# One ScalarE operation as the seed of the inverse root, and an earlier place for tile 0's scaled table

## The chip, the cores and the metric

The program runs on one core of a Trainium2 chip. Its time is the device time of one execution in microseconds (us). Of the kernel before there are three timed runs, with a median of 675.24 us (674.69 to 675.34), and one profiled execution.

The engines are named as the profile names them: PE is TensorE (PEld its weight loads), DVE is VectorE, ACT is ScalarE, POOL is GpSimd, SP is SyncE, which issues most transfers.

## The reference, cut to what matters

```python
def _layernorm(x, axis=-1, eps=1e-5):
    m = jnp.mean(x, axis=axis, keepdims=True)
    v = jnp.var(x, axis=axis, keepdims=True)
    return (x - m) / jnp.sqrt(v + eps)

# x: [1, 2048, 640]; w_r, w_i: [2048, 321]; w_gate, w_up: [640, 1728]; w_down: [1728, 640]
def _A_ref(x, w_r, w_i):                      # spectral filter
    X = jnp.fft.rfft2(x, axes=(-2, -1))
    return jnp.fft.irfft2(X * (w_r + 1j * w_i), s=(S, D), axes=(-2, -1))

def _B_ref(x, w_gate, w_up, w_down):          # gated unit without a nonlinearity
    return ((x @ w_gate) * (x @ w_up)) @ w_down

h  = x + _A_ref(_layernorm(x), w_r, w_i)
h2 = h + _B_ref(_layernorm(h), w_gate, w_up, w_down)
```

## The kernel before, in words

**Stages.** The 2048 rows are held as 16 tiles X[0] to X[15] of 128 x 640. Stage 1 (up to 38.91 us in the profile) is the first layernorm and the first part of the Fourier transform; then come the filter, the inverse transform, and from about 152 us the second layernorm, which overlaps with the inverse transform's end and the gated unit. The gated unit fills the rest, with PE busy nearly all the time.

**Stage 1, tile by tile.** For tile t four things are needed before its matmuls (`s1_mm`, recorded as L252, 14 records a tile). (1) The statistics: mean and variance by `bn_stats` and `bn_aggr` on DVE (L176, L179, L180), or, for eight of the tiles, two passes over the tile on ACT: a sum (L195) and a sum of squares (L196), each followed by an accumulator read. (2) The inverse root r = (v + eps)^-1/2 (`inverse_root`, L201): ACT takes a square root (L205), DVE a reciprocal (L206) as seed, and three small DVE operations (L207 to L209) make one Newton step, r (1.5 - 0.5 r^2 (v + eps)). (3) The folds of the tile: sums and differences of mirrored columns (L229 `odd`, L234, L238, L239 `even`). L234 needs the mean and writes the part that the first matmuls read, L239 the part that the later ones read. (4) The table of cosines and sines scaled by r (`scale_c`, tile name bits): on ACT (L267) for tile 0 and tiles 5 to 15, on DVE (L269) for tiles 1 to 4. So r does not scale the data but the small table that they are multiplied with. ACT also copies the results out of PSUM (L275, L278). POOL makes a few of the odd folds.

**Groups.** The roots are taken for several tiles at once: tile 0, tile 1, tiles 2 and 3, 4 and 5, 6 to 9, 10 and 11, 12 and 13, 14 and 15. The statistics of 0, 2, 3, 12 and 13 come wholly from DVE; for those groups L183 forms v + eps as an operation of its own. Groups with ACT passes get v + eps out of the scaling of the sum of squares (L198). The second layernorm has four groups more (`scale_shift`, L748).

**What sets the order.** Each engine does its instructions in the order in which the program issues them. In the loop over tiles (L318 to L377) that order is written by hand for tiles 0 to 2; from tile 3 on `weave` places the root's steps between the folds by fixed costs. An instruction that waits holds up all behind it on its engine. Tiles are numbered by t; in the instruction lists the data of tile t is x_68 for t = 0, x_69 for t = 1, and so on (x_77 is tile 9, x_78 is tile 10).

Of the kernel before, what the change touches and what calls it, by code (L numbers as in the profile page):

```python
# [11 lines left out]
F32 = mybir.dt.float32  # L12
F32R = mybir.dt.float32r
AF = mybir.ActivationFunctionType
OP = mybir.AluOpType

P = 128
# [23 lines left out]
EPS = 1e-5  # L41
# [37 lines left out]
def tile_spectral_glu(ctx: ExitStack, tc: tile.TileContext, x, wre, wim, wgu, wlast, wdown, wdlast,  # L79
                      cc, ci, fmain, frem, imain, irem, mm, out):  # L80
    nc = tc.nc

    keep = ctx.enter_context(tc.tile_pool(name="keep", bufs=1))
    work = ctx.enter_context(tc.tile_pool(name="work", bufs=8))
    small = ctx.enter_context(tc.tile_pool(name="small", bufs=5))
# [3 lines left out]
    tt, act = nc.vector.tensor_tensor, nc.scalar.activation  # L89
# [10 lines left out]
    def bank(tag, bufs=2):  # L100
        return pools["y" if tag in ("im2", "ir2") else "a"].tile([P, 512], F32, tag=tag, name=tag, bufs=bufs)
# [10 lines left out]
    def wk(shape, name):  # L112
        return work.tile(shape, F32, tag="wk", name=name)
# [51 lines left out]
    def moments(ts, junk=None, total=None, k=0):  # L165
        n = len(ts)
        m2 = small.tile([P, n], F32, tag="m2", name="m2")
        ve = small.tile([P, n], F32, tag="ve", name="ve")

        def statistics(ts):  # L170
            n = len(ts)
            mv = small.tile([P, n, 2], F32, tag="mv", name="mv")
            fs, late = [], None
            for i, t in enumerate(ts):
                st = small.tile([P, 2, 6], F32, tag="st", name="st")
                fs.append(lambda st=st, t=t: nc.vector.bn_stats(st[:, 0], X[t][:, 0:320]))  # L176
                if late:
                    fs.append(late)
                fs.append(lambda st=st, t=t: nc.vector.bn_stats(st[:, 1], X[t][:, 320:640]))  # L179
                late = lambda st=st, i=i: nc.vector.bn_aggr(mv[:, i], st)  # L180
            fs.append(late)
            fs.append(lambda: nc.vector.tensor_scalar(m2[:, 0:n], mv[:, :, 0], 2.0, None, op0=OP.mult))
            fs.append(lambda: nc.vector.tensor_scalar(ve[:, 0:n], mv[:, :, 1], EPS, None, op0=OP.add))  # L183
            return fs

        if junk is None:
            return m2, ve, statistics(ts)
        first = statistics(ts[:k]) if k else []
        sq = small.tile([P, n], F32, tag="sq", name="sq")
        fs = []  # L190
        if total is not None:
            fs.append(lambda: nc.vector.tensor_scalar(m2, total, 2.0 / D, None, op0=OP.mult))
        for i, t in list(enumerate(ts))[k:]:
            if total is None:
                fs.append(lambda t=t, i=i: act(junk[i], X[t], AF.Identity, scale=2.0 / D, accum_out=m2[:, i:i + 1]))  # L195
            fs.append(lambda t=t, i=i: act(junk[i], X[t], AF.Square, bias=m2[:, i:i + 1], scale=-2.0,  # L196
                                           accum_out=sq[:, i:i + 1]))
        fs.append(lambda: nc.vector.tensor_scalar(ve[:, k:n], sq[:, k:n], 0.25 / D, EPS, op0=OP.mult, op1=OP.add))  # L198
        return m2, ve, first + fs

    def inverse_root(ve, r, n):  # L201
        sd = small.tile([P, n], F32, tag="sd", name="sd")
        w = small.tile([P, n], F32, tag="w", name="w")
        return [
            lambda: act(sd, ve, AF.Sqrt),  # L205
            lambda: nc.vector.reciprocal(r, sd),  # L206
            lambda: nc.vector.scalar_tensor_tensor(w, r, -0.5, r, op0=OP.mult, op1=OP.mult),  # L207
            lambda: tt(w, w, ve, op=OP.mult),
            lambda: nc.vector.scalar_tensor_tensor(r, w, 1.5, r, op0=OP.add, op1=OP.mult),  # L209
        ]  # L210

# [2 lines left out]
    def front(ts, k):  # L214
        n = len(ts)
        r = small.tile([P, n], F32, tag="r", name="r")
        junk = [fold[:, o:o + D] for o in (NR * 1026, NR * 1026 + D)]
        m2, ve, fs = moments(ts, junk * 2 if k < n else None, k=k)
        for i, t in enumerate(ts):
            SC[t] = r[:, i:i + 1], m2[:, i:i + 1]  # L220
        return fs, inverse_root(ve, r, n)

    def folded(t):
        o = t % NR * 1026
# [39 lines left out]
    def scale_c(t):  # L264
        CR[t] = crs[t % 4]
        if t in SCALE_ON_ACT:
            act(CR[t], cct, AF.Copy, scale=SC[t][0])  # L267
        else:
            nc.vector.tensor_scalar(CR[t], cct, SC[t][0], None, op0=OP.mult)  # L269
# [4 lines left out]
    def s1_rest(t):  # L274
        act(at(rest, t), PS1[t][1][:, 0:P].rearrange("p (g m) -> p g m", g=32), AF.Copy)  # L275
# [14 lines left out]

    warm = wk([P, P], "warm")
    nc.vector.memset(warm, 0.0)
    pw = bank("re")
    for n in range(16):
        nc.tensor.matmul(pw[:, 0:P], warm, warm, start=True, stop=True)
    f0, c0 = front((0,), 1)
    f1, c1 = front((1,), 0)
    for f in f0:
        f()
    for ts, when, aside, root in GROUPS:  # L300
        k = len(when)
        fs, cs = front(ts, k)
# [15 lines left out]
    for t in range(NT):  # L318
        if t == 1:
            nc.gpsimd.dma_start(frall, frem)  # L320
        if t >= 1:
            fs = even(t)
            if t + 1 < NT and t + 1 not in ASIDE:
                fs.insert(1, (0.4, lambda: odd(t + 1, nc.vector)))
            if t < AHEAD:
                fs.insert(1 + (t <= 2), (0.2, lambda: scale_c(t)))
            if t == 1:
                fs, (recip, w, *left) = fs[1:], dve[1][0]
                for f in (c1[4], fs[0][1], fs[1][1], recip, fs[2][1], w):
                    f()  # L330
                dve[2].insert(0, left)
            elif t == 2:
                (ww, r), = dve[2]
                for f in (fs[0][1], ww, tail[2].pop(), fs[1][1], r, fs[2][1], fs[3][1]):
                    f()
            else:
                weave(fs, dve[t], t in FOLDS)
            for f in tail[t]:
                f()
            if t < AHEAD - 1:  # L340
                s1_rest(t - 1)
                main = lambda: s1_main(t - 1, PS1[t - 1][0], 0, 4)
                for f in acts[t][:1] + post[t] + ([*acts[t][1:], main] if t < 2 else [main, *acts[t][1:]]):
                    f()
            else:
                s1_main(t - 1, PS1[t - 1][0], 0, 4)
                s1_rest(t - 1)
                for f in post[t]:
                    f()
                if t + 1 in SCALE_ON_ACT:  # L350
                    scale_c(t + 1)
                for f in acts[t]:
                    f()
        else:
            e0 = [f for _, f in even(0)]
            c0[0]()
            for f in (e0[0], c0[1], e0[1], c0[2], c0[3], e0[2], c0[4], *f1[:-1]):
                f()
        if t in FOLDS:
            nc.gpsimd.tensor_copy(small.tile([P, 1], F32, tag="hold", name="hold"), folded(t)[1][:, 383:384])  # L360
            for k in FOLDS[t]:
                odd(k, nc.gpsimd)
        if t >= 1:
            for f in stats[t]:
                f()
            if AHEAD <= t + 1 < NT and t + 1 not in SCALE_ON_ACT:
                scale_c(t + 1)
        else:
            scale_c(0)
            b2a, b2, b3a, a2, b3, a3, m, v = stats[0]  # L370
            for f in (b2a, b2, b3a, b3, a2, f1[-1], acts[0][0], c1[0], *acts[0][1:], even(1)[0][1], a3, c1[1], m, c1[2],
                      v, c1[3]):
                f()
        if t == 0:
            for f in post[0]:
                f()
        s1_mm(t)  # L377
# [370 lines left out]
    def scale_shift(ts, junk, total=None):  # L748
        n = len(ts)
        r = small.tile([P, n], F32, tag="r", name="r")  # L750
        b = small.tile([P, n], F32, tag="b", name="b")
        m2, ve, fs = moments(ts, junk, total)
        cs = inverse_root(ve, r, n)
        cs.append(lambda: nc.vector.scalar_tensor_tensor(b, m2, -0.5, r, op0=OP.mult, op1=OP.mult))
        for i, t in enumerate(ts):
            SC[t] = r[:, i:i + 1], b[:, i:i + 1]
        return fs, cs
# [101 lines left out]
    total = small.tile([P, 8], F32, tag="total", name="total", bufs=1)  # L859
# [6 lines left out]
    for ts in (range(3), range(3, 6), range(6, 8)):  # L866
        n, t0 = len(ts), ts[-1] + 1
        fs, cs = scale_shift(ts, [scrap] * n, total[:, ts[0]:t0])
# [301 lines left out]
    for n, (blk, p) in enumerate(steps):  # L1170
        if p == 6:
# [121 lines left out]
            if blk == 0:  # L1293
                fs, cs = scale_shift(range(8, 16), None)
# [6 lines left out]
        if prev[1] == 6:  # L1301
            fs = [[lambda j=j, prev=prev: down(*prev, j)] for j in range(8)]
            slots = [dict(zip(range(4, 8), fs[0:3] + [fs[3] + fs[4]])), dict(zip((2, 3, 4), fs[5:]))]
        else:
            fs = down_products(*prev, (0, 1)) + down_products(*prev, (2, 3))
# [222 lines left out]
```

## Time and profile before

| | |
|---|---|
| median of three runs | 675.24 us (674.69 to 675.34) |
| the profiled execution, its own time | 674.77 us |
| its span in the profile | 673.0 us |
| PE busy | 662.0 us (98%) |
| PEld busy | 587.0 us (87%) |
| DVE busy | 471.6 us (70%) |
| ACT busy | 322.7 us (48%) |
| POOL busy | 393.6 us (58%) |

The span begins at the first instruction and ends at the last; 1.77 us of the run lie around it. The shares are means over stages that are limited by different engines, so that the stage which the change touches has to be looked at by itself. The granted TensorE clock is at its full level in all 40 slices of the span.

### The profile page before, as it was taken

The page shows a single profiled execution, that of the slowest core. Times are in us where ns is not written, and L with a number is a line of the kernel's source. Part 1 is how long each engine was busy: PE and PEld are TensorE (multiplying, and loading weights), DVE is VectorE, ACT ScalarE, POOL GpSimd, SP SyncE. Part 2 cuts the span into 40 slices and gives each one's busy share as a digit, 9 for nine tenths or more (in the row PEclk, how much of TensorE's full clock was granted, in tenths as well). Part 3 has the DMA queues.
Part 4 walks back from the last instruction along what each step waited for, and adds up shares of the span by engine and source line. Part 5 has one row for each costly group of instructions (what it writes and reads, how often), then busy time and mean ns, then how long its engine had stood idle before and what let it go on. Part 6 is the DMA issues. An engine that isn't in the chain of part 4 may idle for free.

```text
span 673.0 us, 10263 instructions
## 1 busy us (share of the span) xinstructions
PE 662.0 (98%) x3695; PEld 587.0 (87%) x3695; DVE 471.6 (70%) x967; ACT 322.7 (48%) x622; POOL 393.6 (58%) x377
## 2 busy tenths in 40 slices
PE   6999999999999999999999999999999999999997
PEld 6999998887898888888888899888888888888887
DVE  6969996788757868594857567754747575756654
ACT  6977774585525244463626246634434252525220
POOL 3101124650297987878787544188787878787610
PEclk9999999999999999999999999999999999999999
DMA  9639884502212110042332458212002121212004
GB/s 317 226 104 283 242 256 142 170 1 79 78 40 78 40 70 23 27 119 59 96 81 79 98 125 265 79 40 76 11 32 79 40 78 40 79 40 80 1 1 156
DMA packets 48953, 66.12 MB, mean 98 GB/s; under 512 B 24082, under 2 KB 30670, under 8 KB 48774
## 3 DMA queue, kind: packets, MB, share of 16 engines
q1 hardware_dynamic: 48246, 62.91, 30.3%
q0 software_dynamic: 288, 2.16, 0.8%
q8 instruction: 29, 0.48, 0.3%
q10 hardware_dynamic: 368, 0.39, 0.3%
q14 instruction: 22, 0.18, 0.1%
HBM read 54.61 MB, written 10.84 MB: 97 GB/s over the span
## 4 chain that ended last, share of the span: by engine, by line
PE 92%; DMA 4%; DVE 2%; ACT 1%; issue 1%; SPq 0%; DVEq 0%; ACTq 0%
PE e L119 49%; PE d L119 26%; PE eo L119 4%; PE re L119 2%; PE u L455 2%; PE y L119 2%; PE im L119 2%; PE im L507 2%; DMA x<-in_x_dram 2%; PE im L252 1%; DMA bits<-in_mm_dram 1%; PE ir L507 1%; DMA wts<-in_wre_dram 1%; PE y L773 0%; ACT xt L783 0%
## 5 line engine op out<-in xcount | busy, mean ns | idle before, releaser
L119 PE MATMUL e<-xt,wst 128*128 128x512 f32 x864 | 213.2, 391 | 0.0
L119 PEld LDWEIGHTS e<-xt,wst 128*128 128x128 f32 x864 | 159.8, 188 | 30.6
L1047 DVE TENSOR_TENSOR x<-d,x 128x320 f32<-128x320 f32 x280 | 123.4, 484 | 51.6 <-PE d L119 47.5
L119 PE MATMUL d<-wd,ht 128*128 128x320 f32 x832 | 143.6, 308 | 0.0
L119 PEld LDWEIGHTS d<-wd,ht 128*128 128x128 f32 x832 | 131.1, 188 | 7.6
L961 POOL TENSOR_TENSOR wst<-raw,wst 128x1024 fp32r<-128x1024 f32 x23 | 55.5, 2412 | 66.9 <-ACT wst L960 49.0
L119 PE MATMUL e<-t,wst 128*128 128x512 f32 x360 | 94.3, 392 | 0.0
L119 PEld LDWEIGHTS e<-t,wst 128*128 128x128 f32 x360 | 66.3, 188 | 12.6
L119 PE MATMUL d<-wt,ht 128*128 128x320 f32 x360 | 69.5, 310 | 0.0
L977 POOL TENSOR_TENSOR wst<-raw,wst 128x896 fp32r<-128x896 f32 (+1 forms) x46 | 65.1, 1439 | 0.2 <-ACT wst L972 0.2
L119 PEld LDWEIGHTS d<-wt,ht 128*128 128x128 f32 x360 | 57.3, 188 | 2.3
L1063 ACT ACTIVATE ht<-e 128x512 fp32r<-128x512 f32 x44 | 26.4, 600 | 51.4 <-DVE e L1126 25.8
L1102 ACT ACTIVATE h<-e 128x512 f32<-128x512 f32 x24 | 14.3, 596 | 67.2 <-PE e L119 67.2
L1022 DVE TENSOR_TENSOR x<-d,x 128x320 f32<-128x320 f32 x62 | 27.5, 485 | 23.2 <-PE d L119 23.2
L658 ACT ACTIVATE wd<-draw 128x320 fp32r<-128x320 f32 (+1 forms) x30 | 15.7, 558 | 57.5 <-POOL draw L668 54.3
L972 ACT ACTIVATE wst<-raw 128x896 fp32r<-128x896 f32 (+1 forms) x48 | 30.2, 676 | 26.8 <-POOL raw L966 26.0
L119 PE MATMUL e<-xt,wdir 128*128 128x512 f32 x180 | 42.0, 392 | 0.4 <-DVE w L207 0.2
L119 PEld LDWEIGHTS e<-xt,wdir 128*128 128x128 f32 x180 | 33.4, 188 | 8.2 <-ACT xt L783 0.7
L1122 DVE TENSOR_TENSOR e<-e,h 128x512 f32<-128x512 f32 x24 | 16.8, 699 | 30.7 <-PE e L119 17.7
L1066 DVE TENSOR_TENSOR ht<-e,ht 128x512 fp32r<-128x512 f32 x54 | 37.0, 685 | 1.6 <-ACT ht L1063 1.3
L637 POOL TENSOR_TENSOR wd<-draw,wd 128x640 fp32r<-128x640 f32 x8 | 12.5, 1576 | 40.5 <-ACT wd L636 40.5
L1119 ACT ACTIVATE h<-e 128x512 f32<-128x512 f32 x24 | 14.4, 599 | 40.1 <-PE e L119 40.1
(234 smaller groups left out, 1189.4 us busy)
## 6 DMA issues: line engine op xcount, KB each, us to landing
raw<-in_wgu_dram SPq DMA_DIRECT2D x24, 640.0 KB
draw<-in_wdown_dram SPq DMA_DIRECT2D x24, 320.0 KB
wts<-in_wre_dram SPq DMA_DIRECT2D x16, 322.0 KB
x<-in_x_dram SPq DMA_DIRECT2D x15, 320.5 KB
out_dram<-x SPq DMA_DIRECT2D x15, 320.0 KB
bits<-in_mm_dram SPq DMA_DIRECT2D x32, 128.0 KB
wts<-in_wim_dram SPq DMA_DIRECT2D x9, 322.0 KB
zfar<-zr SPq DMA_DIRECT2D x32, 80.0 KB
```

The costliest lines, as they stand in the source:

```text
L119: nc.tensor.matmul(o, l, r, start=start, stop=stop, skip_group_check=True)
L507: nc.tensor.matmul(out, y[:, h, a:b], inv(g, h), start=n == 0, stop=n == len(ys) - 1)
L658: act(o[:, 0, a:a + n], src, AF.Copy)
L961: ptt(wa[:, 1], stage[:, 0:1024], f32(wa[:, 0]), op=OP.subtract)
L972: act(ws[:, 0, o:o + b - a], stage[:, a:b], AF.Copy)
L977: ptt(ws[:, 1, o:o + b - a], stage[:, a:b], f32(ws[:, 0, o:o + b - a]), op=OP.subtract)
L1022: tt(xv, ps[b][:, 0:320], xv, op=OP.add)
L1047: tt(xv, o, xv, op=OP.add)
L1063: act(hop[:, a, 0], src, AF.Copy)
L1066: engine.tensor_tensor(hop[:, a, 1], src, f32(hop[:, a, 0]), op=OP.subtract)
L1119: act(h1, oa, AF.Copy)
L1122: tt(ob, ob, h1, op=OP.add)
```

## The change: what it does

`inverse_root` no longer takes a square root on ACT and a reciprocal on DVE: one ACT operation (`Abs_reciprocal_sqrt`) writes the seed r. The Newton step after it stays. Where a group's statistics come wholly from DVE (tile 0; 2 and 3; 12 and 13; the last group of the second layernorm) ACT reads the variance straight from `mv` and adds eps by a per-partition bias, a new 128 x 1 tile that DVE fills once at the start; L183 is gone there, and the Newton step's second operation becomes one that adds eps as it multiplies. For tile 0 the order is also written anew: its scaled table is issued on ACT between tile 1's two passes instead of behind them, and the last fold of tile 0 comes behind the Newton step.

```diff
+        def wide():
+            if "ve" not in spread_of:
+                spread_of["ve"] = small.tile([P, n], F32, tag="ve", name="ve")
+            return spread_of["ve"]
...
             fs.append(lambda: nc.vector.tensor_scalar(m2[:, 0:n], mv[:, :, 0], 2.0, None, op0=OP.mult))
-            fs.append(lambda: nc.vector.tensor_scalar(ve[:, 0:n], mv[:, :, 1], EPS, None, op0=OP.add))
+            if alone:
+                spread_of["mv"] = mv[:, :, 1]
+                fs.append(lambda: None)
+            else:
+                ve = wide()
+                fs.append(lambda: nc.vector.tensor_scalar(ve[:, 0:n], mv[:, :, 1], EPS, None, op0=OP.add))
             return fs
...
+        if junk is None or k == n:
+            fs = statistics(ts, True)
+            var = spread_of["mv"]
+            return m2, (var, 1.0, lambda w: nc.vector.scalar_tensor_tensor(w, var, EPS, w, op0=OP.add, op1=OP.mult)), fs
...
-    def inverse_root(ve, r, n):
-        sd = small.tile([P, n], F32, tag="sd", name="sd")
+        times = lambda w: tt(w, w, ve, op=OP.mult)
+        return m2, (ve, None, times), first + fs
+
+    def inverse_root(spread, r, n):
+        src, scale, times = spread
         w = small.tile([P, n], F32, tag="w", name="w")
+        root = AF.Abs_reciprocal_sqrt
         return [
-            lambda: act(sd, ve, AF.Sqrt),
-            lambda: nc.vector.reciprocal(r, sd),
+            lambda: act(r, src, root) if scale is None else act(r, src, root, bias=eps, scale=scale),
+            lambda: None,
             lambda: nc.vector.scalar_tensor_tensor(w, r, -0.5, r, op0=OP.mult, op1=OP.mult),
-            lambda: tt(w, w, ve, op=OP.mult),
+            lambda: times(w),
             lambda: nc.vector.scalar_tensor_tensor(r, w, 1.5, r, op0=OP.add, op1=OP.mult),
         ]
...
+    eps = keep.tile([P, 1], F32, name="eps")
+    nc.vector.memset(eps, EPS)
...
             c0[0]()
-            for f in (e0[0], c0[1], e0[1], c0[2], c0[3], e0[2], c0[4], *f1[:-1]):
+            for f in (e0[0], c0[2], e0[1], f1[0], c0[3], c0[4]):
+                f()
+            scale_c(0)
+            for f in (e0[2], f1[1]):
                 f()
...
-            scale_c(0)
```

The instructions of PE, POOL and SP stand in the same order as before. On DVE, from the end of tile 0's statistics to the start of the next ones (line numbers of the changed kernel are 5 to 19 higher), the rows of before are these:

```order
L180 BN_AGGR mv<-st 128x2
L182 TENSOR_SCALAR m_139<-mv 128x1
L183 TENSOR_SCALAR ve<-mv 128x1
L234 SCALAR_TENSOR_TENSOR fold<-x_68,m_139 128x2x161
L206 RECIPROCAL r<-sd 128x1
L238 TENSOR_TENSOR fold<-fold 128x64
L207 SCALAR_TENSOR_TENSOR w<-r 128x1
L208 TENSOR_TENSOR w<-w,ve 128x1
L239 TENSOR_TENSOR fold<-fold 128x2x160
L209 SCALAR_TENSOR_TENSOR r<-w,r 128x1
L176 BN_STATS st<-x_70 128x6
```

and these are the rows of the changed kernel at the same place on DVE:

```order
L185 BN_AGGR mv<-st 128x2
L187 TENSOR_SCALAR m_141<-mv 128x1
L249 SCALAR_TENSOR_TENSOR fold<-x_68,m_141 128x2x161
L222 SCALAR_TENSOR_TENSOR w<-r 128x1
L253 TENSOR_TENSOR fold<-fold 128x64
L199 SCALAR_TENSOR_TENSOR w<-mv,w 128x1
L224 SCALAR_TENSOR_TENSOR r<-w,r 128x1
L254 TENSOR_TENSOR fold<-fold 128x2x160
L181 BN_STATS st<-x_70 128x6
```

Two small operations are gone, and the last fold (128x2x160) stands behind the step that ends r. On ACT, at the start of the program, the rows of before are (x_69 is tile 1, x_72 tile 4, bits the scaled table):

```order
L205 ACT_TABLE_LOAD
L205 ACTIVATE sd<-ve 128x1
L195 ACTIVATE fold,m_146<-x_69 128x640
L196 ACTIVATE fold,sq<-x_69,m_146 128x640
L267 ACTIVATE bits<-cct,r 128x128
L195 ACTIVATE fold,m_165<-x_72 128x640
L205 ACTIVATE sd<-ve 128x1
```

and on ACT of the changed kernel:

```order
L220 ACT_TABLE_LOAD
L220 ACTIVATE r<-mv,eps 128x1
L208 ACTIVATE fold,m_146<-x_69 128x640
L282 ACTIVATE bits<-cct,r 128x128
L209 ACTIVATE fold,sq<-x_69,m_146 128x640
L208 ACTIVATE fold,m_161<-x_72 128x640
L220 ACTIVATE r<-ve 128x1
```

The table has moved ahead of tile 1's second pass; there is one load of activation tables in either program. The third place is DVE around the folds of tiles 9 (x_77) and 10 (x_78); as the piece of before reads:

```order
L198 TENSOR_SCALAR ve<-sq 128x2
L234 SCALAR_TENSOR_TENSOR fold<-x_77,m_171 128x2x161
L206 RECIPROCAL r<-sd 128x2
L229 TENSOR_TENSOR fold<-x_78 128x2x160
L207 SCALAR_TENSOR_TENSOR w<-r 128x2
```

and in the changed kernel, on DVE:

```order
L211 TENSOR_SCALAR ve<-sq 128x2
L249 SCALAR_TENSOR_TENSOR fold<-x_77,m_166 128x2x161
L244 TENSOR_TENSOR fold<-x_78 128x2x160
L222 SCALAR_TENSOR_TENSOR w<-r 128x2
L253 TENSOR_TENSOR fold<-fold 128x64
```

The first instruction that needs ACT's result was the reciprocal, directly behind tile 9's fold; now it is w<-r, one fold later.

## Rows read from the trace of the kernel before

**Rows 1.** Busy time by stretch: us, then PE, PEld, DVE, ACT, POOL, clock, DMA.

```profile
8.93:29.11 20.18, 17.56 (x140) 16.50 (x141) 19.86 (x83) 19.45 (x58) 5.85 (x11) 1.00 0.93 346
29.11:38.91 9.80, 9.79 (x85) 9.77 (x85) 8.21 (x32) 7.77 (x25) 0.00 (x0) 1.00 0.05 15
38.91:108.00 69.09, 68.30 (x473) 62.43 (x472) 60.33 (x89) 51.69 (x121) 14.30 (x33) 1.00 0.76 225
```

**Rows 2.** Waits of PE, whole span, the longest: releaser, us, times, longest.

```profile
PE im L252 <- ACT bits L267: 2.6, 1, 2.6
```

**Rows 3.** Timeline of tile 0: start, us, engine, line, idle before in brackets.

```profile
1.97 1.28 ACT L205 ACT_TABLE_LOAD   x1 [1.97 <-issue]
...
6.46 0.15 DVE L182 TENSOR_SCALAR m<-mv 128x1 f32<-128x1 f32 x1
6.54 0.14 DVE L183 TENSOR_SCALAR ve<-mv 128x1 f32<-128x1 f32 x1
6.71 0.20 ACT L205 ACTIVATE sd<-ve 128x1 f32<-128x1 f32 x1 [3.46 <-DVE ve L183]
6.73 0.56 DVE L234 SCALAR_TENSOR_TENSOR fold<-x,m 128x322 f32<-128x322 f32 x1
...
8.13 0.15 DVE L209 SCALAR_TENSOR_TENSOR r<-w,r 128x1 f32<-128x1 f32 x1
8.20 0.49 DVE L176 BATCH_NORM_STATS2 st<-x 128x6 f32<-128x320 f32 x1
...
8.50 0.39 ACT L267 ACTIVATE bits<-cct,r 128x128 f32<-128x128 f32 x1
...
8.93 1.86 PE L252 MATMUL im<-bits,fold 128*128 128x128 f32 x14 [2.60 <-ACT bits L267]
```

**Rows 4.** Timeline of tiles 1 and 2: a reciprocal, tile 2's table on DVE, ACT's copy.

```profile
11.47 0.16 DVE L206 RECIPROCAL r<-sd 128x2 f32<-128x2 f32 x1
11.54 0.47 DVE L239 TENSOR_TENSOR fold<-fold 128x320 f32<-128x320 f32 x1
...
13.82 0.29 DVE L269 TENSOR_SCALAR bits<-cct,r 128x128 f32<-128x128 f32 x1
...
16.12 0.28 ACT L275 ACTIVATE rest<-im 128x128 f32<-128x128 f32 x1 [0.18 <-PE im L252]
```

**Rows 5.** Timeline around tiles 9 and 10, on ACT, DVE and PE.

```profile
25.08 0.25 ACT L196 ACTIVATION_READ_ACCUMULATOR fold<-x,m 128x1 f32 x1
25.38 0.16 DVE L198 TENSOR_SCALAR ve<-sq 128x2 f32<-128x2 f32 x1
25.45 0.55 DVE L234 SCALAR_TENSOR_TENSOR fold<-x,m 128x322 f32<-128x322 f32 x1
25.80 0.27 ACT L205 ACTIVATE sd<-ve 128x2 f32<-128x2 f32 x1
26.11 0.17 DVE L206 RECIPROCAL r<-sd 128x2 f32<-128x2 f32 x1
26.19 0.49 DVE L229 TENSOR_TENSOR fold<-x 128x320 f32<-128x320 f32 x1
28.34 0.63 DVE L234 SCALAR_TENSOR_TENSOR fold<-x,m 128x322 f32<-128x322 f32 x1
29.11 3.19 PE L252 MATMUL im<-bits,fold 128*128 128x128 f32 x26 [0.55 <-DVE mv L180]
```

**Rows 6.** Groups by line on ACT: busy us, mean ns; L196 has a per-partition bias.

```profile
L196 ACT ACTIVATE fold<-x,m 128x640 f32<-128x640 f32 x9 | 7.6, 841 | 0.1
L195 ACT ACTIVATE fold<-x 128x640 f32<-128x640 f32 x9 | 6.7, 740 | 0.0
```

**Rows 7.** Timeline at the end of the inverse transform.

```profile
151.65 0.16 DVE L206 RECIPROCAL r<-sd 128x2 f32<-128x2 f32 x1
151.72 0.47 DVE L729 TENSOR_TENSOR q<-eo,s 128x322 f32<-128x322 f32 x1
152.34 3.65 PE L119 MATMUL e<-xt,wdir 128*128 128x512 f32 x15 [0.25 <-DVE w L207]
```

More of the change, by code (lines that the diff above doesn't have):

```diff
@@ L167, in moments, with statistics @@
         m2 = small.tile([P, n], F32, tag="m2", name="m2")
-        ve = small.tile([P, n], F32, tag="ve", name="ve")
-        def statistics(ts):
+        spread_of = {}
+        def wide():
+            if "ve" not in spread_of:
+                spread_of["ve"] = small.tile([P, n], F32, tag="ve", name="ve")
+            return spread_of["ve"]
+        def statistics(ts, alone):
             n = len(ts)
@@ L182, in statistics @@
             fs.append(lambda: nc.vector.tensor_scalar(m2[:, 0:n], mv[:, :, 0], 2.0, None, op0=OP.mult))
-            fs.append(lambda: nc.vector.tensor_scalar(ve[:, 0:n], mv[:, :, 1], EPS, None, op0=OP.add))
-            return fs
-        if junk is None:
-            return m2, ve, statistics(ts)
-        first = statistics(ts[:k]) if k else []
+            if alone:
[4 more added lines that the diff above has]
+                fs.append(lambda: nc.vector.tensor_scalar(ve[:, 0:n], mv[:, :, 1], EPS, None, op0=OP.add))
+            return fs
+        if junk is None or k == n:
+            fs = statistics(ts, True)
+            var = spread_of["mv"]
+            return m2, (var, 1.0, lambda w: nc.vector.scalar_tensor_tensor(w, var, EPS, w, op0=OP.add, op1=OP.mult)), fs
+        first = statistics(ts[:k], False) if k else []
         sq = small.tile([P, n], F32, tag="sq", name="sq")
+        ve = wide()
         fs = []
@@ L198, in moments @@
         fs.append(lambda: nc.vector.tensor_scalar(ve[:, k:n], sq[:, k:n], 0.25 / D, EPS, op0=OP.mult, op1=OP.add))
-        return m2, ve, first + fs
-    def inverse_root(ve, r, n):
-        sd = small.tile([P, n], F32, tag="sd", name="sd")
+        times = lambda w: tt(w, w, ve, op=OP.mult)
+        return m2, (ve, None, times), first + fs
+    def inverse_root(spread, r, n):
+        src, scale, times = spread
         w = small.tile([P, n], F32, tag="w", name="w")
+        root = AF.Abs_reciprocal_sqrt
         return [
-            lambda: act(sd, ve, AF.Sqrt),
-            lambda: nc.vector.reciprocal(r, sd),
+            lambda: act(r, src, root) if scale is None else act(r, src, root, bias=eps, scale=scale),
+            lambda: None,
             lambda: nc.vector.scalar_tensor_tensor(w, r, -0.5, r, op0=OP.mult, op1=OP.mult),
-            lambda: tt(w, w, ve, op=OP.mult),
+            lambda: times(w),
             lambda: nc.vector.scalar_tensor_tensor(r, w, 1.5, r, op0=OP.add, op1=OP.mult),
@@ L217, in front @@
         junk = [fold[:, o:o + D] for o in (NR * 1026, NR * 1026 + D)]
-        m2, ve, fs = moments(ts, junk * 2 if k < n else None, k=k)
+        m2, spread, fs = moments(ts, junk * 2 if k < n else None, k=k)
         for i, t in enumerate(ts):
             SC[t] = r[:, i:i + 1], m2[:, i:i + 1]
-        return fs, inverse_root(ve, r, n)
+        return fs, inverse_root(spread, r, n)
     def folded(t):
@@ L751, in scale_shift @@
         b = small.tile([P, n], F32, tag="b", name="b")
-        m2, ve, fs = moments(ts, junk, total)
-        cs = inverse_root(ve, r, n)
+        m2, spread, fs = moments(ts, junk, total)
+        cs = inverse_root(spread, r, n)
         cs.append(lambda: nc.vector.scalar_tensor_tensor(b, m2, -0.5, r, op0=OP.mult, op1=OP.mult))
```

## The prediction

> **What bounds the kernel now.** I read the busy shares first, then the time by stretch, the waits of PE, and the timeline of the start. PE is busy 98% of the span, and from 29.11 us on it hardly stops: 9.79 us of 9.80 to the end of stage 1, and 68.30 of 69.09 in the filter after it [rows 1]. So what this change can give has to be won before 29.11 us, as an earlier start of PE's unbroken work, and what is won there should carry to the end unless something later does not move with PE. In the 20.18 us before, PE is busy only 17.56, while DVE is busy 19.86 and ACT 19.45 [rows 1]: two engines run nearly full and feed the third. The longest wait of PE in the whole span is 2.6 us for tile 0's scaled table [rows 2], and its last one in stage 1 ends at 29.11 us, 0.55 us long [rows 5]. That row puts the wait down to L180, but tile 10's matmuls do not read it; they read the fold L234 of 28.34 + 0.63 = 28.97 us, and start 0.14 us later. So the number to work out is how much earlier that fold starts.
>
> **Tile 0.** L182 runs at 6.46, L183 at 6.54, the fold L234 at 6.73 [rows 3]. Without L183 the fold needs only the mean, ready at 6.46 + 0.15 = 6.61, and starts at about 6.64. The new seed reads the variance, which is there when L182 starts. This form of the operation is not in the trace. Its nearest row is the square root on one column, 0.20 us [rows 3]; a per-partition bias makes a pass over 640 columns 841 - 740 = 101 ns longer [rows 6]. So I take 0.30 us; the bounds are 0.20 and the 0.39 us of the scaled table, which has such an operand on 128 columns [rows 3]. It ends at 6.76 to 6.85, behind the 0.56 us fold which DVE does meanwhile: whatever it costs within these bounds, it is hidden. After the fold's end at 7.20 four operations are left: a short fold, and w, its product and r, each about 0.15 us and each waiting for the one before. From 7.20 I get r at about 7.71 (before: 8.13 + 0.15 = 8.28), the last fold at 7.63, and the next statistics at 8.03 instead of 8.20 [rows 3]. DVE gains 0.17 us here.
>
> The table is the larger gain, and it is worth nothing by itself. With r at 7.71 and the table ahead of tile 1's second pass, it runs from 7.75 to 8.14, and PE starts at 8.18 instead of 8.93 [rows 3]. But PE then waits for tile 1's table, which DVE makes after the same number of steps as before; the 0.75 us become a longer wait there. The price on ACT is that tile 1's second pass, queued behind the table, ends about 0.4 us later. Nobody waits for it: it ends at about 9.0 (8.14, a pass of 0.84 less the overlap, and the read of the sum), while DVE from 8.03 on first does four statistics of some 0.4 us each.
>
> **Tiles 1 to 8.** A removed small operation frees its place in DVE's queue, not its 0.16 us duration: the reciprocal at 11.47 is followed at 11.54, the one at 26.11 at 26.19 [rows 4, 5], so 0.07 to 0.08 us each, since neighbours overlap. [...] Between tiles 0 and 2 one such place counts (L183 of tiles 2 and 3 stood in a chain of waits, which stays), so tile 2's table, at 13.82 [rows 4], comes 0.17 + 0.07, about 0.25 us earlier, and so do PE's tile 2 and ACT's copy of its result. That copy, at 16.12 after a wait of 0.18 us for PE [rows 4], is where ACT takes over the gain: from there to 29 us ACT is busy without a gap. The two bias operands before it, 0.1 us each, are covered by that and an earlier wait. So ACT from there on is 0.25 us early, and no more, since it has lost nothing else.
>
> **Tiles 9 and 10.** DVE by itself would gain 0.25 plus two more places, about 0.40, by the time it reaches L198 of 25.38. But that reads the sum which ACT's accumulator read of 25.08 delivers at 25.33 [rows 5]: there is no slack, so it moves by ACT's 0.25 us. Then comes the second gain. DVE waited for the square root, which ended at 25.80 + 0.27 = 26.07; the reciprocal started at 26.11, the next fold at 26.19 [rows 5]. Without both, that fold follows L234 directly, about 0.09 us before its end at 25.45 + 0.55 = 26.00, at 25.91: 0.28 us. The first reader of the seed is now behind that fold, at about 26.06, and the seed is there at 25.82, so no new wait appears. From here on DVE is 0.25 + 0.28 = 0.53 us early, up to tile 10's fold. PE had finished tile 9 at 29.11 - 0.55 = 28.56 even before, so nothing keeps it from starting tile 10 at 28.58 instead of 29.11.
>
> **The rest.** In tiles 10 to 15 DVE and ACT gain further, but PE has almost no gaps to close there [rows 1]: 0 to 0.1 us, taken as 0.05. In the second layernorm a reciprocal of 0.07 us stands ahead of a fold (L729) whose end at 152.19 lets PE start at 152.34 after 0.25 us of waiting [rows 7]: 0.07 us. The other three groups there lie beside a busy PE and give nothing. The fill of eps lies in DVE's wait for the first data: nothing.
>
> The sum: 0.53 + 0.05 + 0.07 = 0.65 us. From the profiled execution's own 674.77 us that makes 674.12; that execution lies 0.47 us under the median of the runs shown, and from the median of 675.24 us the forecast is 674.6 us. Bounds of the sum: nothing, if none of it is on the path that counts; and, if each of the six reciprocals and two L183 before tile 10 were worth its whole 0.16 us, 1.3 us.
>
> **Rivals.** *ACT sets the pace, and the gain stops half way.* For it: 19.45 us busy of 20.18, and L198 that follows ACT's sum within 0.05 us [rows 1, 5]. Against it: the 0.18 us wait of ACT for PE, by which ACT can follow [rows 4]. Then only the 0.28 us at 26.11 and the 0.07 later are left: 0.35, so 674.9 us.
>
> *ACT is later than before, and the kernel slower.* One mechanism: the table now waits at the head of ACT's queue for r, and ACT's next pass starts 0.08 us later than before (from 7.75 a table of 0.39 and a pass of 0.84, less 0.1 of overlap each, make 8.87, where before it followed the table of 8.50 at about 8.79); the two bias operands add 0.2 us. If ACT does not win this back in its waits for PE, its sum at 25.33 comes 0.28 us later, and that eats exactly the 0.28 us at the reciprocal; tile 9's own table follows on ACT behind the square root of 25.80 and ends at about 26.4, when PE, at some 1.6 us a tile (9.80 for six [rows 1]) and done with tile 9 at 28.56, needs it within a few tenths; that delays PE by up to 0.3 us. This decides from the point on where ACT's copy of 16.12 no longer waits for PE. Time: 675.24 + 0.3 = 675.5 us.
>
> [...]
>
> *More is won.* If DVE alone sets the pace up to 29 us, the whole-duration bound above holds at most: 1.3 us, so 673.9 us.
>
> **How the numbers follow.** The forecast has 0.62, the half gain 0.18, ACT later 0.10, more won 0.08, another set of tables 0.02. About 0.2% of the time, 1.35 us, is what a measurement of this kernel can tell from no change; the forecast, the half gain and nearly all of ACT later lie within it. Faster by more takes the last bit of "more won", and chips and runs that differ by as much as the three runs' 0.65 us: 0.09. Slower by more takes the other set of tables or something unseen after PE: 0.06. Within: 0.85. The range reaches from 673.5 (1.3 us won, and a run at the low end) to 675.8 (ACT later, at the high end).
>
> **What would show it.** PE's first stage 1 matmul at about 8.2 us and its wait before tile 1 longer; tile 2's table at about 13.6; the fold behind tile 9's at about 25.7, with no wait for the seed ahead of w; PE unbroken from about 28.6; the end of PE's stage 1 at 38.3 instead of 38.91, and the same distance at 152 us and at the end. It is wrong if ACT's copy of tile 2 does not come earlier, if PE's last wait in stage 1 ends at 29 us or later, or if a new wait after 39 us takes the half microsecond back.

## The result and the profile after

The changed kernel takes 675.79 us (median of 22 runs, 675.59 to 676.44), the kernel before, on the same chip, 674.92 us (22 runs, 674.36 to 676.23): a ratio of 1.0013, interval 1.0007 to 1.0019. It is slower by 0.87 us where I forecast 0.65 us less. The span goes from 673.0 to 673.9 us, PE's busy time from 662.0 to 663.6 us (1.6 more) with the same 3695 matmuls, DVE's from 471.6 to 470.8.

At the start, events came in the order forecast, within 0.15 us of the times forecast. The timeline of the changed kernel, in the columns of [rows 3]; L220 is the new seed, L249 the fold that was L234, L282 the scaled table, L181 the next statistics:

```profile
6.43 0.29 ACT L220 ACTIVATE r<-mv,eps 128x1 f32<-128x1 f32 x1 [3.18 <-DVE mv L185]
...
6.70 0.56 DVE L249 SCALAR_TENSOR_TENSOR fold<-x,m 128x322 f32<-128x322 f32 x1
...
7.81 0.40 ACT L282 ACTIVATE bits<-cct,r 128x128 f32<-128x128 f32 x1 [0.37 <-DVE r L224]
8.09 0.49 DVE L181 BATCH_NORM_STATS2 st<-x 128x6 f32<-128x320 f32 x1
...
8.26 0.38 PE L267 MATMUL im<-bits,fold 128*128 128x128 f32 x1 [1.59 <-ACT bits L282]
```

PE starts at 8.26 instead of 8.93 us and then waits for tile 1 (its longest wait there is now 1.5 us, for the table that DVE makes). Around tile 9, answering to [rows 5] (L211 was L198, L244 the fold L229, L222 the first step behind the seed):

```profile
25.25 0.17 DVE L211 TENSOR_SCALAR ve<-sq 128x2 f32<-128x2 f32 x1
25.33 0.56 DVE L249 SCALAR_TENSOR_TENSOR fold<-x,m 128x322 f32<-128x322 f32 x1
...
25.70 0.27 ACT L220 ACTIVATE r<-ve 128x2 f32<-128x2 f32 x1
...
25.81 0.48 DVE L244 TENSOR_TENSOR fold<-x 128x320 f32<-128x320 f32 x1
...
26.21 0.15 DVE L222 SCALAR_TENSOR_TENSOR w<-r 128x2 f32<-128x2 f32 x1
...
28.73 0.79 PE L267 MATMUL im<-bits,fold 128*128 128x128 f32 x5 [0.54 <-ACT fold L209]
```

The wait for the seed is gone, and tile 10 starts on PE at 28.73 instead of 29.11. PE's stage 1 ends at 38.34 instead of 38.91 us. After that there is no new wait. PE's waits from 38 us to the end (waited for: us in total, times, longest) are those of before, one by one:

```profile
PE eo L119 <- ACT qm L552: 0.5, 1, 0.5
PE ir L526 <- DVE qr L559: 0.3, 1, 0.3
PE e L119 <- DVE ht L926: 0.2, 1, 0.2
PE e L119 <- DVE w L222: 0.2, 1, 0.2
```

And yet the lead is lost. Matched one by one, PE's matmuls start 0.56 us earlier than before at 150 us and 0.64 at 182; from there the gap shrinks steadily through the gated unit: 0.17 earlier at 320 us, 0.21 later at 420, 0.96 later at 655. The profile's chain of the work that ended last shows how. Pieces of it (start, us, count) of the kernel before:

```profile
316.14 2.06 PE e L119 x9
...
319.52 6.83 PE e L119 x30
...
356.56 6.83 PE e L119 x30
...
655.40 14.09 PE d L119 x96
```

and of the changed kernel:

```profile
315.95 2.08 PE e L119 x9
...
319.34 6.88 PE e L119 x30
...
356.55 6.88 PE e L119 x30
...
656.36 14.09 PE d L119 x96
```

The same 30 matmuls take 6.88 instead of 6.83 us, the same nine 2.08 instead of 2.06: about 2 ns each on average, on an engine that does not wait there, at the full granted clock (1.00). One turn of the pattern takes 356.55 - 319.34 = 37.21 instead of 37.04 us. The groups of instructions by form (busy us, mean ns of one | idle; the records of neighbouring matmuls overlap, so that the mean of one is longer than the 227 ns from start to start, 6.83 us for 30), before:

```profile
L119 PE MATMUL e<-xt,wst 128*128 128x512 f32 x864 | 213.2, 391 | 0.0
...
L119 PE MATMUL e<-t,wst 128*128 128x512 f32 x360 | 94.3, 392 | 0.0
```

and after:

```profile
L119 PE MATMUL e<-xt,wst 128*128 128x512 f32 x864 | 214.2, 392 | 0.0
...
L119 PE MATMUL e<-t,wst 128*128 128x512 f32 x360 | 94.6, 392 | 0.0
```

No instruction was added or moved there. What did change is where data lies. The new tile eps, one number in each partition, takes 32 bytes of SBUF in the built program, and all that is allocated behind it moves by 32 bytes: the part of w_down in the tile wt (194848 to 194880), a sum of operands, t3 in the program (202528 to 202560), and the small working tiles (206624 to 206656). xt, the other weights and ht stay. The rows print t3 as `t`, but also another tile, t12, which stays: of the 360 matmuls of e<-t only 72 read t3. All the matmuls named here read the first tile behind the arrow as moving data and the second as weights.

### The profile page after: what moved, and what is told of

Read it like the earlier page. It is cut to its first block, busy times and chain, and to the rows that moved or that the text cites. A ratio compares the mean times of both kernels' runs of the same rounds, so it can differ in the third digit from the quotient of the medians.

```text
span 673.9 us, 10248 instructions
## 1 busy us (share of the span) xinstructions
PE 663.6 (98%) x3695; PEld 587.6 (87%) x3695; DVE 470.8 (70%) x952; ACT 322.8 (48%) x622; POOL 393.0 (58%) x377
## 4 chain that ended last, share of the span: by engine, by line
PE 93%; DVE 3%; ACT 2%; issue 1%; DMA 1%; DVEq 0%; ACTq 0%
PE e L119 49%; PE d L119 26%; PE eo L119 4%; PE re L119 2%; PE u L474 2%; PE y L119 2%; PE im L119 2%; PE im L526 2%; PE im L267 2%; PE ir L526 1%; DMA x<-in_x_dram 1%; ACT s L293 1%; ACT fold L209 0%; ACT fold L208 0%; PE y L792 0%
## 5 line engine op out<-in xcount | busy, mean ns | idle before, releaser
L119 PE MATMUL e<-t,wst 128*128 128x512 f32 x360 | 94.6, 392 | 0.0
```

The source lines that it names most:

```text
L119: nc.tensor.matmul(o, l, r, start=start, stop=stop, skip_group_check=True)
```

## The experiments

My theory was then that the place of wt and t3 in SBUF, the on-chip memory, costs PE the time. The rivals: something else that the change does (fewer DVE operations, the other order); the place of the working tiles, which DVE, ACT and POOL use. The table sums up what the sections below show. "Drift" is how much later, against the kernel before, PE's same matmul starts at the end of a stretch than at its beginning; each from two pairs of starts. The ratio is to the kernel before on the same chip.

| kernel | moved by | drift 182 to 420 us | drift 450 to 655 us | ratio of times |
|---|---|---|---|---|
| after | wt, t3, working tiles: 32 bytes | +0.85 | +0.74 | 1.0013 (1.0007 to 1.0019) |
| e1 after, eps elsewhere | none of these | 0.00 | 0.00 | 0.9987 (0.9978 to 0.9996) |
| e2 before, with a pad | as after | +0.84 | +0.78 | 1.0025 (1.0016 to 1.0034) |
| e3 after, wider eps | as after, but 64 | +0.70 | +0.67 | 1.0007 (0.9999 to 1.0016) |
| e5 after, wider eps | as after, but 128 | +0.46 | +0.45 | 1.0004 (0.9995 to 1.0013) |
| e4 e1 with a pad | working tiles: 32 | -0.01 | 0.00 | 0.9991 (0.9983 to 1.0) |
| e6 e1 with a pad | t3, working tiles: 32 | +0.46 | +0.42 | 0.9999 (0.9991 to 1.0008) |
| e7 e1, old table place | none of these | 0.00 | +0.01 | 0.9988 (0.9979 to 0.9997) |

The stretch from 420 to 450 us is left out, since the matmuls e<-xt,wdir there differ between profiles of the same kernel: of two profiles of one kernel (e9 and e11) one has a step of 0.65 us there, the other none.

**e1: eps behind all else.** The changed kernel, with eps in the last pool:

```diff
-    eps = keep.tile([P, 1], F32, name="eps")
+    eps = small.tile([P, 1], F32, tag="eps", name="eps", bufs=1)
```

> The changed kernel with eps in the pool of small tiles, which lies behind all others, so that wt, t3 and the working tiles stand at the same addresses as before. Theory of place (PE's matmuls of the gated unit are 0.2 us per 37 us slower because eps moved those tiles by 32 bytes): the 0.57 us won by 38 us stays to the end, time 0.5 to 0.7 us under the kernel before, the changed kernel's 1.5 us loss between 185 and 656 us gone. Theory of order (the loss comes from the new order and the earlier start of PE, whatever the addresses): as the changed kernel, 0.9 us over the kernel before.

674.35 us (11 runs) beside 675.21 for the kernel before (32 runs), 0.86 us less, and the chain has the old pieces again:

```profile
319.11 6.83 PE e L119 x30
...
356.16 6.83 PE e L119 x30
...
655.19 14.09 PE d L119 x96
```

Nothing but the place of eps, and of what moves with it, differs from the changed kernel, so that place costs the 1.6 us. The change itself wins about what was forecast, and this kernel beats both. At 655 us this profile is only 0.21 us ahead of the kernel before: its first data came 0.15 us later (first statistics at 5.45 instead of 5.30), and 0.19 went in the stretch that the table leaves out. Counted from the first statistics, PE is 0.51 us ahead at the end of stage 1, where the changed kernel is 0.53.

**e2: the tile without the change.** The kernel before, with a tile of the same size at eps's place, filled once and never read:

```diff
+    pad = keep.tile([P, 1], F32, name="pad")
+    nc.vector.memset(pad, EPS)
```

> The kernel before with a tile of 4 bytes per partition at eps's place and one DVE fill of it at the start, nothing else. Theory of place: stage 1 as before (PE's second stage from 38.9 us), then the same slow drift, 1.4 to 1.6 us over the kernel before. Theory of order: same time as before within 0.2 us.

676.99 us, 1.78 us more than before, and the pieces of the changed kernel:

```profile
320.16 6.88 PE e L119 x30
...
357.37 6.88 PE e L119 x30
```

So the cost needs nothing of the new seed and nothing of the new order.

**e4 and e6: which tile.** Both are e1 with an unused tile of 4 bytes in the first pool, in e4 behind t3 (only the working tiles move), in e6 between wt and t3 (t3 and the working tiles move):

```diff
+    pad = keep.tile([P, 1], F32, name="pad")     # e4: ahead of banks("a", "pthree")
...
+        if g == 1:
+            pad = keep.tile([P, 1], F32, name="pad")     # e6
```

> As with eps in the pool of small tiles, but with an unused tile of 4 bytes behind t3, so that wt and t3 keep their addresses and the working tiles alone move by 32 bytes. If PE's own reads of wt and t3 are what got slower: 0.5 to 0.7 us under the kernel before. If the working tiles (which DVE, ACT and POOL read and write) are what counts: 0.9 us over it. A split between: part of each. Theory of order: 0.9 us over it.

> eps in the pool of small tiles, and an unused tile of 4 bytes between wt and t3: t3 (operand of some of PE's matmuls) and the working tiles move by 32 bytes, wt keeps its address. The working tiles alone cost nothing that the trace shows, so: if t3 is what counts, most of the 1.5 us comes back, at 0.5 to 0.9 us over the kernel before, with slower matmuls at e<-ht,wst, e<-t,wst and those behind them; if wt counts, 0.5 to 0.9 us under it, and the d<-wt,ht matmuls at their old pace.

e4 takes 674.73 us and does not drift: the working tiles are out. e6 takes 675.13 us and drifts by 0.88 us in all, over half of the changed kernel's 1.59; in time it is only 0.06 us over the kernel before, where 0.5 to 0.9 was expected if t3 was what counts. The rest, 0.7 us, is left for wt (by subtraction; wt was not moved alone). In e6's trace the 72 matmuls that read ht ahead of t3 are unchanged (20.5 us before), those that read `t` have the changed kernel's 94.6 us:

```profile
L119 PE MATMUL e<-t,wst 128*128 128x512 f32 x360 | 94.6, 392 | 0.0
...
L119 PE MATMUL e<-ht,wst 128*128 128x512 f32 x72 | 20.5, 393 | 0.0
```

Matched one by one in the table's two stretches, the loss does not lie only where the moved tile is read. Of e6's 0.87 us, 0.23 fall on the matmuls that read t3 (three at a time), 0.58 on the seven directly behind each three, whatever they read, and 0.06 on all others. From e6 to the changed kernel, 0.71 us more, 0.13 fall on the matmuls that read wt and 0.60 on the nine behind each group of them. So in the piece of 30 matmuls above, which ends with 24 that read xt, the first seven of these 24 are 37 ns longer in all and the other 17 not at all. All but 0.01 of the 0.96 us that e<-xt,wst lost in the two stretches lies in such places, though xt did not move.

**e3 and e5: another distance.** The changed kernel with eps 16 and 32 numbers wide, of which one is used:

```diff
-    eps = keep.tile([P, 1], F32, name="eps")
+    eps = keep.tile([P, 16], F32, name="eps")[:, 0:1]     # e5: 32
```

> The changed kernel with eps made 64 bytes long, so that the tiles behind it move by 64 instead of 32 bytes. Theory of place, in the form that the start within 64 bytes counts (which a move of 64 leaves as before): 0.5 to 0.7 us under the kernel before. In the form that any move from the old place costs, or that the start within 128 bytes counts: over it, by anything up to 0.9 us or more. Theory of order: 0.9 us over it.

> The changed kernel with eps made 128 bytes long: the tiles behind it move by 128 bytes. So far a move of 32 and one of 64 bytes both cost about 1.5 us. If what counts is the place within 128 bytes: no drift between 185 and 656 us, 0.6 to 0.9 us under the kernel before. If it is the place within a longer unit, or relative to tiles that did not move: drift of 0.5 to 1.6 us, at 0.2 us under to 0.9 us over the kernel before.

676.0 and 675.41 us: a step of 64 bytes costs 1.4 us of drift, one of 128 bytes 0.9. So a start that is unchanged within 64 or within 128 bytes does not bring the old pace back. A step of 256 was not run with the whole kernel.

**e7: the table's place.** e1 with tile 0's order and the place of its table as before:

```diff
-            for f in (e0[0], c0[2], e0[1], f1[0], c0[3], c0[4]):
-                f()
-            scale_c(0)
-            for f in (e0[2], f1[1]):
+            for f in (e0[0], c0[1], e0[1], c0[2], c0[3], e0[2], c0[4], *f1[:-1]):
                 f()
...
+            scale_c(0)
```

> eps in the pool of small tiles, the new seed, but tile 0's table and Newton step in the order of before. By the prediction the earlier table is worth nothing behind tile 1: PE's first matmul of stage 1 at about 8.7 us instead of 8.3, but its second stage starts, counted from the first statistics, within 0.1 us of where it does with the earlier table (33.0 us behind them instead of 33.6 before). Rival (the earlier order at tile 0 carries the gain): 0.2 us or more later than that. Time about 0.5 to 0.8 us under the kernel before either way.

674.34 us (10 runs) and 675.07 for the kernel before: the ratio of e1 within 0.0001. PE's first matmul of stage 1 comes late again (8.74 us), but tile 2's table (L284) does not:

```profile
8.74 1.67 PEld L267 LDWEIGHTS im<-bits,fold 128*128 128x128 f32 x14 [2.66 <-ACT bits L282]
...
13.72 0.29 DVE L284 TENSOR_SCALAR bits<-cct,r 128x128 f32<-128x128 f32 x1
```

The earlier table is worth nothing by itself, as forecast.

**e9 and e11: the wait without the new seed.** The kernel before, with the reciprocal one fold later for the roots from tile 9 on:

```diff
-        dve[root].append(cs[1:])
+        dve[root].append([lambda: None] * (root > 8) + cs[1:])
```

> The kernel before with one thing changed: from the root of tiles 10 and 11 on, the reciprocal stands one fold later on DVE. Both square root and reciprocal stay. By the prediction DVE's wait for ACT ahead of that reciprocal, 0.2 us at 26.1 us, is a term of its own: PE's last wait of stage 1 ends about 0.2 us earlier (23.6 us behind the first statistics instead of 23.8), the second stage starts 0.2 us earlier, time 0.2 us under the kernel before, which the timing hardly tells. Rival (that wait is given back by another one): no difference in the trace.

e9 takes 675.21 us beside 675.07, a ratio of 0.9998 (0.9989 to 1.0007); in its profile the granted clock was 0.91 from 9 to 29 us and 1.00 from 0 to 9 and from 29 to 39 us (PE busy 18.56 us of the 20; in e11 17.38, with 1.00 in all three stretches), so that the trace of e11, the same kernel again, is the one to read:

> Once more the kernel before with the reciprocal behind one more fold from tile 9 on; in the first profile of it the granted clock was 0.91 between 9 and 29 us, so that PE's times there could not be compared. Theory: VectorE's wait for the square root at 26.1 us goes, the fold behind it starts about 0.25 us earlier against L198, and PE's tile 10 starts 0.2 to 0.3 us earlier than in the kernel before, counted from the first statistics; 28.8 instead of 29.1 us, and so to the end: 674.9 us. Rival: ScalarE's sum sets the pace of tile 10, and PE starts it within 0.1 us of 29.1: 675.2 us.

675.02 us beside 674.75 (1.0001, 0.999 to 1.0012). Its timeline, to be read beside [rows 5]:

```profile
25.24 0.16 DVE L198 TENSOR_SCALAR ve<-sq 128x2 f32<-128x2 f32 x1
...
25.78 0.48 DVE L229 TENSOR_TENSOR fold<-x 128x320 f32<-128x320 f32 x1
...
26.18 0.15 DVE L206 RECIPROCAL r<-sd 128x2 f32<-128x2 f32 x1
...
26.84 0.49 DVE L239 TENSOR_TENSOR fold<-fold 128x320 f32<-128x320 f32 x1
...
28.88 0.79 PE L252 MATMUL im<-bits,fold 128*128 128x128 f32 x5 [0.54 <-DVE mv L180]
```

The fold L229 now follows L198 after 0.54 instead of 0.81 us: the wait is gone. But from L229 to L239 it takes 1.06 us instead of 0.88, since the chain of four small operations that wait for each other, 0.2 us from start to start, now starts there; PE's tile 10 comes 28.88 - 25.24 = 3.64 us behind L198 instead of 3.73. So only 0.09 us of 0.27 is left, and the rival's 0.1 us held, though for this reason and not for ACT's sum. In the changed kernel the chain is one operation shorter, 0.87 us from L244 to the same fold, and nothing is given back.

**e10 and e12: the pitch by itself.** PE alone, in blocks of 96 matmuls, each with a weight load, that read their moving data in turns of three from X and from T. In e10 T is moved from block to block, then all comes again with DVE and POOL busy on other tiles (ACT's operations came too late: 0.00 us of them in the row of the second part below):

```diff
+    PHASES = ((0, 0), (0, 8), (0, 16), (0, 24), (0, 32), (0, 64), (0, 0), (56, 56))
+    for x, t in PHASES:
+        stream(x, 1024 + t, 512, 96)
```

> This kernel leaves the whole computation out. PE runs blocks of 96 matmuls; in each, three that read an operand X at a fixed place are followed by three that read an operand T, whose place is moved from block to block by 0, 32, 64, 96, 128, 256 and again 0 bytes against X, and in a last block both are moved together; five blocks of 320 columns follow with 0 to 128 bytes. Then all blocks come once more while VectorE, ScalarE and GpSimd run operations on other tiles without a pause. In the changed kernel the 864 + 360 matmuls that were slower there lost about 1.0 us, some 1 ns for each, or 5 to 14 ns where a matmul stands behind one that reads another tile. Theory: the pitch of PE alone depends on the place of what it reads, so the moved blocks of the first part are longer than the unmoved by 96 x 1 ns or more, 0.1 to 0.4 us of about 21.6 us each. Rival: PE alone does not care, and the loss comes from other engines that use SBUF at the same time: then the blocks of the first part agree within 0.02 us and only those of the second part differ with the place. Third: neither part differs; then the loss needs something of the real kernel (its strides, its weights, its transfers).

Blocks of the first part, then one of the second (stretch; its us, then busy us of PE, PEld, DVE, ACT, POOL with counts, the neighbour's matmul counted too, and the granted clock):

```profile
29.34:51.09 21.75, 21.75 (x97) 18.03 (x96) 0.00 (x0) 0.00 (x0) 0.00 (x0) 1.00 0.00 0
51.10:73.27 22.17, 22.17 (x97) 18.04 (x96) 0.00 (x0) 0.00 (x0) 0.00 (x0) 1.00 0.00 1
...
140.25:162.05 21.80, 21.80 (x97) 18.02 (x96) 0.00 (x0) 0.00 (x0) 0.00 (x0) 1.00 0.00 1
183.82:206.21 22.39, 22.39 (x97) 18.05 (x96) 0.00 (x0) 0.00 (x0) 0.00 (x0) 1.00 0.00 1
298.53:320.71 22.18, 22.18 (x97) 18.02 (x96) 21.14 (x31) 0.00 (x0) 20.93 (x17) 1.00 0.01 1
```

These are T moved by 0, 32 and 256 bytes, both moved by 224, and T by 32 once more in the second part; by 64, 96 and 128 bytes a block takes 22.33, 22.35 and 22.29 us. PE alone has the effect, 0.4 to 0.6 us in 96 matmuls, and DVE and POOL beside it, busy 21.14 and 20.93 us of 22.18, change it by 0.02 us at most. A step of 256 costs 0.05 us, and moving X and T together by 224 costs most, 0.64 us, so a distance between X and T is not needed for the loss. e12 moves both together, by 32 bytes from block to block:

```diff
+    for c in range(20):
+        stream(8 * c, 1024 + 8 * c, 512, 96)
+    for c in range(20):
+        stream(8 * c, 1024 + 8 * c, 320, 96)
```

> This kernel leaves the whole computation out. As in the first part of e10 PE works alone on blocks of 96 matmuls, but both operands X and T are moved together, from block to block by 32 bytes, 20 blocks of 512 columns and then 20 of 320; the first block has them at 288 bytes behind a multiple of 512, where the kernel before has the operands of its gated unit. In e10 a block took 21.76 us there, 22.40 with both moved by 224 bytes, and 21.81 with T alone moved by 256. Theory: the place within some number of bytes counts, so the times repeat with a period (256 or 512 bytes: the block moved by 512 is at 21.76 again, and the one moved by 256 at 21.8 to 21.9), and the blocks moved by 32 to 224 take 22.2 to 22.9 us, about twice e10's 0.43 to 0.59 us of loss where only T was moved. Rival: a fast place is one where X and T lie alike, so that all blocks but the one moved by 224 are at 21.8. The loss that both have in common says by how much the kernel before is better off than at other places; if a block is faster than 21.7 us, the kernel before has a better place to go to.

```profile
29.75:51.51 21.76, 21.76 (x97) 18.02 (x96) 0.00 (x0) 0.00 (x0) 0.00 (x0) 1.00 0.00 0
51.52:73.91 22.39, 22.39 (x97) 17.99 (x96) 0.00 (x0) 0.00 (x0) 0.00 (x0) 1.00 0.00 1
73.92:95.89 21.97, 21.97 (x97) 18.03 (x96) 0.00 (x0) 0.00 (x0) 0.00 (x0) 1.00 0.00 1
...
207.98:229.73 21.75, 21.75 (x97) 18.02 (x96) 0.00 (x0) 0.00 (x0) 0.00 (x0) 1.00 0.00 0
386.20:407.96 21.76, 21.76 (x97) 18.02 (x96) 0.00 (x0) 0.00 (x0) 0.00 (x0) 1.00 0.00 0
...
474.77:488.83 14.06, 14.06 (x97) 14.06 (x96) 0.00 (x0) 0.00 (x0) 0.00 (x0) 1.00 0.00 0
488.84:502.91 14.07, 14.07 (x98) 14.07 (x97) 0.00 (x0) 0.00 (x0) 0.00 (x0) 1.00 0.01 1
```

The rows are steps of 0, 32, 64, 256 and 512 bytes with 512 columns, and of 0 and 32 with 320. The times repeat every 256 bytes, as the first theory said: 21.76 us unmoved, 21.75 moved by 256 bytes and 21.76 by 512, and the seven blocks between take 156.46 us both times. The fast place is 32 bytes behind a multiple of 256, at 21.76 us or 227 ns a matmul; the second best, 64 bytes on, takes 21.98, the six others 22.39 to 22.48, up to 234 ns a matmul. No block is faster. That the loss would be about twice that of T alone did not come true: it is 0.63 to 0.72 us at six places, and at 64 bytes 0.22, where T alone lost 0.57. So the place of each operand by itself is not the whole account; that X and T lie differently costs too. The weights lay at one place in all blocks of e10 and e12, it too 32 bytes behind a multiple of 256. Whether the place of the moving data counts by itself or against that of the weights, no run tells apart. In the kernel before, xt (59680), wt and t3 all start 32 bytes behind a multiple of 256; the new tile took wt and t3 away from there. Blocks of 320 columns take the same 14.07 to 14.08 us at all places (in e10, where T moves alone, 13.98 to 14.09).

## Why the prediction was wrong, step by step

**The step that failed** is one sentence: "The fill of eps lies in DVE's wait for the first data: nothing." It is true of the instruction (0.06 us at 0.95 us, ahead of DVE's wait of 4.25 us for the first data), and I took it for the whole price of eps. The tile's place was not in the sum, and it costs 1.6 us. With that term the sum comes out: -0.65 + 1.6 = +0.95, and measured were +0.96 us at 655 us (0.64 ahead at 182, then 0.85, 0.01 and 0.74 lost) and +0.87 us in the medians. e1, which has the change without the term, is 0.86 us below the kernel before, in an interval of 0.3 to 1.5 that holds the 0.65.

**The sentence "what is won there should carry to the end unless something later does not move with PE"** named the condition, but I looked for it only among waits; PE at 98% busy has no slack to hide a slower pitch, the time from one matmul's start to the next. The test I gave, "a new wait after 39 us", would not have found it: the list of waits is unchanged; PE's busy time (1.6 us more) shows that there is a loss, and the starts of the same matmuls, matched one by one, show where.

**Tile 0** was right in its shape: seed 0.29 us (taken: 0.30), table at 7.81 (7.75), PE at 8.26 (8.18), next statistics at 8.09 (8.03). That the table is worth nothing by itself was right (e7).

**The 0.25 us through ACT** was too large. L211 comes at 25.25 instead of 25.38, and 0.04 of that is first data that arrived earlier in this execution (first statistics at 5.26 instead of 5.30): 0.09 us. Tile 2's table came at 13.72, not at about 13.6: the place of L183 of tiles 2 and 3 brought nothing there.

**The 0.28 us at the reciprocal** was nearly right: from L198 to the fold 0.81 us before, 0.56 after, 0.25. e11 adds that it is the operation, and not the wait alone, that has to go.

**Tiles 10 to 15**, taken at 0.05, gave 0.18: PE is 0.39 us early at 33.8 us and 0.56 at 35.4, won in two places, 0.07 at 34.1 and 0.11 at 35.2 us. The profile of before records no wait of PE there; what gave way stays open. So 0.53 + 0.05 became 0.38 + 0.18, of which 0.04 is the earlier first data, and the end of stage 1 at 38.34 us stands beside a forecast of 38.3: two errors in the terms nearly cancel. The 0.07 us at 152 us fits (0.56 early at 150 us, 0.64 at 182), but is not shown: the other traces with the new seed and a full clock gain 0.01 to 0.09 there, and that of e11, without it, 0.04.

**The rivals.** "ACT is later than before" did not come: its copy of tile 2 is at 16.02 instead of 16.12, without a wait. "The half gain" and "more is won" are ruled out by the 0.56 us at the end of stage 1. For the 0.02 of another set of tables there is no run that shows what a second load would do: the trace of the changed kernel holds one load on ACT, of 1.28 us at 1.97 us, as that of before. The 0.87 us lie within the 1.35 that I took for what a measurement can tell, which had 0.85 of the chances; but 22 runs of each kernel tell it from nothing (1.0007 to 1.0019). A loss from "something unseen after PE" was named only in the 0.06 for slower by more, and had no time of its own. That the time was just within the range is luck: its upper end stood for another cause.

## What to carry to other kernels

A new tile can have two prices: its instructions (here one of 0.06 us in a wait), and the shift of all that is allocated behind it (here 1.6 us); compare the addresses of matmul operands in the built programs before and after, and put small new tiles into the last pool (e1: no drift). Where PE is busy all the time, a list of waits need not show a loss, as here: match the same matmuls of two traces and look at whether their distance in time grows. And an operation in a chain of short ones that wait for each other cost its step in the chain where it was moved to as well, so that moving it won less than removing it (0.09 us against 0.25).

## What the runs showed of the hardware

With the weights at one place, the pitch of 512-column matmuls depended on where their moving data starts in SBUF, with a period of 256 bytes: 227 ns at the best of eight places, up to 234 ns at the worst, on PE alone with a granted clock of 1.00 (e12). That is a difference of up to 3% at the same columns and the same clock. The loss also falls on the matmuls behind: in e6 the seven behind each three that read t3 lost 0.58 us, those that read it 0.23, and all others 0.06.

Several things stay open. The sizes do not match in detail: in e10 T alone costs more at 64 and 128 bytes (22.33 and 22.29 us) than at 32 (22.19), while the real kernel loses less there (1.4 and 0.9 us than 1.6). PE alone shows next to nothing at 320 columns (14.07 to 14.08 us a block at all places, e12), and wt is read by matmuls of 320 columns; of the 0.7 us that are put down to it, 0.6 fall on the matmuls behind them, nearly all of 512 columns, a mixture that e10 and e12 do not have. The place of the weights was never moved alone. Which part of the memory or of PE's reads sets the period, no run shows.
